# Down stage of a transformer block: the pending pair inside the plain product's first tile, and fewer operand sums in front of two snaps

## The chip, the core and the metric

The kernel runs on one core of one Trainium2 chip. The time is device time in microseconds (us) of one execution. Most executions of one kernel lie within a few us of each other. Engines: PE is the tensor engine (matmuls), PEld its weight loads, DVE the vector engine, ACT the scalar engine; SP only issues transfers here.

## The reference

A pre-LayerNorm block: linear attention, then a gated feed-forward part. Only the last product matters here, `h @ W_down` with h of 2048 x 3584 and W_down of 3584 x 1024:

```python
x = A_x
h = x + _A_ref(_layernorm(x), A_wqkv, A_wo)           # linear attention
# ... gate = relu(x @ W_gate); up = x @ W_up; h = gate * up   (feed-forward)
h2 = h + einsum("bsf,fd->bsd", h, W_down)             # the down stage
```

## The kernel before

The down stage replaces one 2x2 block product by seven products of block sums (a Strassen-Winograd scheme), in two levels. The outer level has seven steps, n = 0 to 6. Steps 0 and 5 are *plain*: four tiles of the output, two halves of 14 matmuls each. Steps 1, 2, 3, 4 and 6 are cut once more into seven groups m1 to m7 of 28 matmuls of 128x256. The groups of one step need sums of operand blocks, made on DVE: s1 to s4 from the activations (128x3584, 1.94 us from start to start) and t1 to t4 from the weights (128x1792, 1.0 us). The profile names their outputs xs, xd, x (from s) and ws, wd, w (from t).

A step's sums wait in a Python list, `queue`, while the program is built; `pop()` puts the next one into DVE's instruction stream. So where `pop()` stands decides what DVE does in which order.

```python
queue.extend((op, f.__name__, f) for f in (t1, s1, s2, t2, s4, s3, t3, t4))

def snap(nm, s, j):     # copies PSUM tile A (plus a base) away; until then PE may not add to A again
    add(out=st[nm][:], in0=view("A"), in1=base[s][:, :, cols(j)], op=ALU.add)
```

Within a step m1, m6, m7 and m4 accumulate into the same PSUM tile A, one on top of another, and a snap saves A after m1, m6 and m7. So m6 waits for the first snap, m7 for the second, m4 for the third. m4 and m3 of a step are issued in the next step: they are the *pending pair* of its forerunner, `prv`.

```python
for n in range(1, len(OUTER)):          # OUTER steps; step 0 is done before
    if op["k"] in INNER:                # a seven-product step
        cur["m1"]()
        if prv:
            prv["11"](); pop()
        cur["s1"]()                     # first snap
        cur["m2"]()
        if prv: prv["m4"]()
        late_x()
        cur["00"]()                     # first output
        pop()
        if prv:
            prv["10"](); prv["m3"]()
        late_w()                        # loads; queues the sums of the next step
        pop()
        cur["m6"]()
        if prv: prv["01"]()
        pop()
        ...
        cur["m5"]()
        cur["s2"]()                     # second snap
        ...
        pop(2)
        cur["m7"]()
        ...
        pop(2)
        cur["s3"]()                     # third snap
        prv = cur
    else:                               # the plain step, n = 5
        for p in range(4):
            ps = acc(...)
            plain_mm(ps, n, p, 0)
            plain_mm(ps, n, p, 1)
            if p == 0 and prv:
                prv["11"](); prv["m4"](); late_x(); prv["10"](); prv["m3"](); late_w(); prv["01"]()
                load_h(op["k"], 1)
            # drain ps: put = two adds and a store, then one add into u2
            ...
            pop(2)
        prv = None
```
(The code is shortened; statements are joined on one line here.)

## Time and profile before

| | before |
|---|---|
| median of the first three runs | 755.6 us (755.51 to 757.81) |
| PE busy, share of the profiled span of 755.9 us | 96% |
| down stage: start of m1 of step 1 to the end of the last DVE operation | 612.23 to 752.69 = 140.46 us |
| PE waits in that stage | 2.11 and 2.64 us |

The timeline view of PE shows the stage as groups back to back. Columns: start in us, length in us, engine, line, operation, output <- inputs, shapes, count; in brackets the idle time before it and what ended it. A length runs to the modelled end of the group's last matmul: groups listed with 3.22 us start 3.06 us apart. A wait in brackets is counted from that modelled end, so a stop costs PE 0.16 us more than the wait listed. These are m6, m5 and m7 of step 1 and the group after, then m2 and m6 of step 6 and the half group after:

```profile
618.34 3.22 PE L1105 MATMUL accA<-ws,xs 128*128 128x256 f16 x28
621.40 3.22 PE L1105 MATMUL accY<-ws,xd 128*128 128x256 f16 x28
626.73 4.88 PE L1105 MATMUL accA<-w,xd 128*128 128x256 f16 x28 [2.11 <-DVE snap L1111]
631.45 3.22 PE L1105 MATMUL accA<-wd,x 128*128 128x256 f16 x28
...
728.99 3.22 PE L1105 MATMUL accX<-wd,x 128*128 128x256 f16 x28
734.85 4.88 PE L1105 MATMUL accA<-ws,xs 128*128 128x256 f16 x28 [2.64 <-DVE snap L1111]
739.57 1.69 PE L1131 MATMUL accX<-ws,xs 128*128 128x256 f16 x14
```

PE stops twice, both times for a snap, and after each stop one group takes 4.88 us in place of 3.22. The timeline view of DVE says why the snaps were late:

```profile
620.41 1.08 DVE L1022 TENSOR_TENSOR ws<-wd 128x1792 f16<-128x1792 f16 x1
621.41 2.02 DVE L1035 TENSOR_TENSOR xs<-x 128x3584 f16<-128x3584 f16 x1
623.52 2.03 DVE L1038 TENSOR_TENSOR xs<-xs,x 128x3584 f16<-128x3584 f16 x1
625.46 1.22 DVE L1111 TENSOR_TENSOR snap<-accA,u 128x1024 f32<-128x1024 f32 x1
...
730.45 1.22 DVE L1278 TENSOR_TENSOR u<-accY,u 128x1024 f32<-128x1024 f32 x1
731.58 1.08 DVE L1029 TENSOR_TENSOR wd<-wd 128x1792 f16<-128x1792 f16 x1
732.58 1.08 DVE L1032 TENSOR_TENSOR ws<-wd,ws 128x1792 f16<-128x1792 f16 x1
733.58 1.22 DVE L1111 TENSOR_TENSOR snap<-accA,u 128x1024 f32<-128x1024 f32 x1
```

Both snaps had their source long before: the first one's m6 ended at about 621.4, the second one's m1 at about 729. Between stand sums that nobody waits for at that moment; ahead of the second snap stand also the drains of the plain step's last tile (the last of them, from 730.45, is shown). DVE ran what stands in its stream in that order: the first snap's source was ready at 621.4 and the snap ran at 625.46, in its place behind the sums.

The waits view (total us, times, longest) has one line for PE in the stage, and the chain of waits (start, length) begins with the two sums of the second place:

```profile
PE accA L1105 <- DVE snap L1111: 4.8, 2, 2.6
```
```profile
731.66 1.00 DVE wd L1029
732.66 1.00 DVE ws L1032
733.66 1.14 DVE snap L1111
734.81 0.04 issue
734.85 4.88 PE accA L1105 x28
```

The stretches view gives, for each stretch of time, its length, the busy time of PE, PEld, DVE, ACT and POOL, then the granted PE clock, the DMA share and GB/s:

```profile
624.60:626.70 2.10, 0.02 (x1) 0.00 (x0) 2.10 (x3) 0.00 (x0) 0.00 (x0) 1.00 1.03 411
626.70:631.50 4.80, 4.77 (x29) 3.65 (x29) 4.80 (x4) 0.00 (x0) 0.00 (x0) 0.64 0.55 216
631.50:695.60 64.10, 64.10 (x590) 57.45 (x588) 53.20 (x44) 0.00 (x0) 0.00 (x0) 1.00 0.82 296
...
732.10:734.80 2.70, 0.11 (x1) 0.00 (x0) 2.70 (x3) 0.00 (x0) 0.00 (x0) 1.00 0.88 283
734.80:739.60 4.80, 4.75 (x29) 3.61 (x29) 1.92 (x2) 0.00 (x0) 0.00 (x0) 0.64 0.40 127
```

After each stop the granted clock is 0.64 on average over the following group; the trace's clock records show a stretch of 3.413 us at 0.5 in each.

### The profile page before, as it was taken

To read this page: it belongs to the slowest core of one execution; us is meant where nothing else is said; L and a number is where in the kernel's file an instruction comes from. 1 tells how busy PE (TensorE), PEld (TensorE's weight loads), DVE (VectorE), ACT (ScalarE), POOL (GpSimd) and SP (SyncE) were. 2 spreads that over 40 slices of the span, in tenths; PEclk is the share of its full clock that TensorE was granted. 3 is DMA by queue.
4 is the path that set the end of the run, shared out by engine and by line. 5 is a ranking of instruction groups with operands and counts; after the bars stand their busy time and mean duration, and the time that the engine had idled before them with its cause. 6 is when DMAs were issued, how large, how long until landed. Compare 5 with 4: busy or idle time off the path is not lost. (4 is left out here: it accounts for less than half of the span.)

```text
span 755.9 us, 10599 instructions
## 1 busy us (share of the span) xinstructions
PE 727.9 (96%) x3967; PEld 384.2 (51%) x4020; DVE 568.2 (75%) x1023; ACT 324.7 (43%) x596; POOL 5.9 (1%) x44
## 2 busy tenths in 40 slices
PE   8999999999889989999999999999999998999987
PEld 3444555444344434444444444444444477888556
DVE  6997654876886766778778787887776398995695
ACT  4785653878767644444344444434344110000000
POOL 0000000000000000000000000000000000000000
PEclk9999999999999999999999999999999999999999
DMA  9756003089857526165638368585482596987722
GB/s 321 167 125 153 0 1 112 1 188 218 186 144 178 135 74 202 35 185 140 200 110 237 112 194 252 194 253 179 144 302 96 189 385 244 360 295 281 238 98 56
DMA packets 146579, 132.03 MB, mean 175 GB/s; under 512 B 50912, under 2 KB 128096, under 8 KB 146528
## 3 DMA queue, kind: packets, MB, share of 16 engines
q1 hardware_dynamic: 135392, 123.23, 53.7%
q10 hardware_dynamic: 11136, 8.13, 3.4%
q8 instruction: 31, 0.51, 0.3%
q14 instruction: 20, 0.16, 0.1%
HBM read 79.95 MB, written 39.85 MB: 158 GB/s over the span
## 5 line engine op out<-in xcount | busy, mean ns | idle before, releaser
L783 ACT ACTIVATE gu<-gu 128x512 bf16<-128x512 bf16 x72 | 45.4, 630 | 131.7 <-DVE gu L782 127.3
L778 ACT COPY snap<-accA 128x1024 f32<-128x1024 f32 x72 | 72.4, 1008 | 37.1 <-PE accA L773 37.1
L536 PE MATMUL attn<-wo_mem,oT 128*128 128x512 bf16 x247 | 58.7, 385 | 4.1 <-DVE o_sb L516 3.3
L773 PEld LDWEIGHTS <-tg 128*128 128x128 f16 x384 | 37.6, 98 | 45.3
L773 PEld LDWEIGHTS <-tu 128*128 128x128 f16 x384 | 37.6, 98 | 45.3
L782 DVE TENSOR_TENSOR gu<-accY,snap 128x1024 bf16<-128x1024 f32 x36 | 43.9, 1219 | 9.8 <-ACT snap L778 9.8
L153 ACT COPY u<-Aq 128x512 f32<-128x512 f32 x56 | 32.3, 582 | 44.0 <-PE Aq L297 20.4
L782 DVE TENSOR_TENSOR gu<-accX,snap 128x1024 bf16<-128x1024 f32 x36 | 43.8, 1218 | 7.3 <-PE accX L773 4.7
L773 PE MATMUL accA<-hn,tg 128*128 128x512 f16 (+1 forms) x192 | 49.3, 379 | 0.0
L773 PE MATMUL accA<-hn,tu 128*128 128x512 f16 (+1 forms) x192 | 49.3, 379 | 0.0
L1105 PEld LDWEIGHTS <-x 128*128 128x128 f16 (+1 forms) x448 | 43.8, 98 | 5.5
L773 PEld LDWEIGHTS <-wg 128*128 128x128 bf16 x288 | 28.2, 98 | 34.9 <-issue 1.1
L773 PEld LDWEIGHTS <-wu 128*128 128x128 bf16 x288 | 28.2, 98 | 34.0
L536 PEld LDWEIGHTS <-oT 128*128 128x128 bf16 x256 | 25.3, 99 | 36.0 <-issue 8.5
L1105 PEld LDWEIGHTS <-xs 128*128 128x128 f16 x280 | 28.2, 101 | 6.7 <-issue 2.8
L297 PEld LDWEIGHTS <-xT 128*128 128x128 bf16 (+1 forms) x192 | 18.6, 98 | 24.5 <-issue 3.2
L786 DVE TENSOR_TENSOR hq<-gu 128x512 bf16<-128x512 bf16 x48 | 20.3, 422 | 14.3 <-ACT gu L783 14.2
L516 DVE TENSOR_TENSOR o_sb<-nd,rd 128x384 bf16<-128x384 f32 (+1 forms) x48 | 22.8, 506 | 8.6 <-ACT rd L515 7.5
L1111 DVE TENSOR_TENSOR snap<-accA,u 128x1024 f32<-128x1024 f32 x16 | 19.5, 1218 | 11.1 <-PE accA L1105 11.1
L538 DVE SCALAR_TENSOR_TENSOR x_res<-attn,x_res 128x512 bf16<-128x512 f32 x32 | 22.0, 688 | 7.6 <-PE attn L536 7.5
L934 PEld LDWEIGHTS <-x 128*128 128x128 bf16 (+1 forms) x168 | 16.4, 98 | 19.8
L773 PE MATMUL accA<-hn,wg 128*128 128x512 bf16 x73 | 23.3, 379 | 2.0 <-DVE gu L702 0.8
(232 smaller groups left out, 1417.0 us busy)
## 6 DMA issues: line engine op xcount, KB each, us to landing
x<-x_dram SPq DMA_DIRECT2D x17, 896.0 KB, 8.4
x_dram<-hq SPq DMA_DIRECT2D x28, 512.0 KB, 3.0
wg<-in_B_W_gate_dram SPq DMA_DIRECT2D x14, 512.0 KB, 5.2
wu<-in_B_W_up_dram SPq DMA_DIRECT2D x14, 512.0 KB, 7.5
wraw<-in_B_W_down_dram SPq DMA_DIRECT2D x14, 512.0 KB, 4.9
x_dram<-hq SPq DMA_DIRECT2D x28, 256.0 KB, 2.4
t_dram<-wt SPq DMA_DIRECT2D x28, 256.0 KB, 2.3
xd<-x_dram SPq DMA_DIRECT2D x6, 896.0 KB, 6.5
```

The source lines that it names most:

```text
L153: nc.scalar.copy(out=snaps[nm, v], in_=A[v][:])
L297: nc.tensor.matmul(ps[:], lhsT=left[m - 1][:, kc, r + v * P:r + (v + 1) * P], rhs=right[m - 1][:, kc, :], start=(start and kc == 0), stop= ...
L516: nc.vector.tensor_tensor(out=ov[:, c0:c0 + n], in0=ndv[:, :, 0:P].rearrange("p k (h e) -> p k h e", h=HPC), in1=rd[:, 0:n, :].unsqueeze(3 ...
L536: nc.tensor.matmul(ps[:], lhsT=st["oT"][:, c, :], rhs=wo_sb[:, c, j * NW:(j + 1) * NW], start=(c == 0), stop=(c == KC - 1))
L538: nc.vector.scalar_tensor_tensor(out=h_sb[:, j * NW:(j + 1) * NW], in0=ps[:], scalar=1.0, in1=h_sb[:, j * NW:(j + 1) * NW], op0=ALU.mult, ...
L773: nc.tensor.matmul(ps[:, v, :], lhsT=w[v][n - 1][:, kc, :], rhs=left[n - 1][:, kc, :], start=(t is not None and kc == 0), stop=(kc == KH - ...
L778: nc.scalar.copy(out=st[nm][:], in_=halves(st["A"]))
L782: add(out=g[:], in0=halves(st[nm]), in1=st[base][:], op=ALU.add)
L783: nc.scalar.activation(out=g[:, 0, :], in_=g[:, 0, :], func=ACT.Relu)
L786: add(out=out[q], in0=st[q][:, 0, :], in1=st[q][:, 1, :], op=ALU.mult)
L1105: nc.tensor.matmul(pv[:, tt, :], lhsT=left(m)[:, f, tt * P:(tt + 1) * P], rhs=right(m)[:, f, :], start=(t is not None and f == 0 and tt % ...
L1111: add(out=st[nm][:], in0=view("A"), in1=base[s][:, :, cols(j)], op=ALU.add)
```

## The change

Its intent: let the two snaps run as soon as PE has filled A. (a) In a step without a forerunner two `pop()` fall away. (b) In the plain step PE does half of the first tile, then the pending pair, then the other half. (c) One sum is popped before the first tile's drain, and none after the last tile.

```diff
             late_w()
-            pop()
+            if prv:
+                pop()
             cur["m6"]()
             if prv:
                 prv["01"]()
-            pop()
+                pop()
...
                 plain_mm(ps, n, p, 0)
-                plain_mm(ps, n, p, 1)
                 if p == 0 and prv:
...
                     prv["01"]()
                     load_h(op["k"], 1)
+                    pop()
+                plain_mm(ps, n, p, 1)
...
-                pop(2)
+                pop(2 if p < 3 else 0)
```

No instruction is added or removed. On PE only m4, m3 and the second half tile of step 5 change places; on DVE sums, snaps and drains do.

## The prediction

The sum: 3.8 us for (a) and 4.5 us for (b) with (c), together the 8.3 us of the walk.

> **What bounds it.** The tensor engine (PE), 96% busy on the page; in the down stage (591 us to the end) the timeline shows groups of 28 matmuls back to back, 3.06 us each, seven per step. PE stops twice. (1) First seven-product step: group m7 waits 2.11 us, to 626.73, for the snap (vector engine, DVE) of 625.46, though its source m6 had ended at 621.4: the operand sums ws, xs, xs (1.00, 2.02, 2.03 us) stood in front of it. (2) Last step: m6 waits 2.64 us, to 734.85, for the first snap of 733.58, behind the plain product's last drain and two sums wd, ws (731.58 to 733.58). The chain of waits begins with these sums. Each stop also costs afterwards: the next group takes 4.88 us where its like take 3.22; the stretches view gives granted clock 0.64 there, 1.00 around. [...]two stretches of 3.413 us at 0.5. From group start to group start the stops cost 6.99-3.06 = 3.93 and 7.52-3.06 = 4.46 us: 8.4 us, 1.1%, all on the critical path.

> **What changes.** Nothing is added or removed; order moves.
> (a) In steps without a forerunner (first and last of the seven-product kind) two sums fewer stand before the second snap. In the first only ws (1.0) remains: the snap runs at about 621.5 to 622.7, and m7 goes at 624.46 unhindered. Sums run about one place later through the next three steps.
> (b) In the plain step PE runs half the first tile, then the pending pair, then the other half. This wins no PE time; but the pair's two outputs drain about 3 us earlier, in DVE idle time (4.89 us before the snap at 695.84, 5.89 before the drain at 704.94).
> (c) That room lets one sum (ws) run before the first tile's drain, and the last tile queues none; of eight sums seven run there, the eighth after the last step's first snap and output.

> **Size.** I walked the PE, DVE and load queues forward with the traced durations; the same walk over the old order gives the waits as 1.98 and 2.93 us (traced 2.11, 2.64). New order: no PE wait in the stage, the last step's first snap done 1 us before m6 needs it, the end 8.3 us earlier. Loads start up to 4 us earlier and land, in the walk, over 2 us before use. Part (a) is worth about 3.8 us, (b) with (c) about 4.5, nearly additive.

> **Prediction: 747.4 us**, 8 in 10 between 746.0 and 750.5. Faster by over 2%: 0.01; within 2%: 0.98; slower by over 2%: 0.01.

> **What would show it.** PE's idle before these two groups gone; both at 3.2 us; before the end only one half-clock stretch (at 203 us) left; these snaps at about 621.5 and 726; all up to 620 us unchanged; the tail after PE's end unchanged (about 4 us).

> **What would make it wrong.** DVE has little slack in the second to fourth seven-product steps: with PE 4 us earlier, the second step's second snap ends only about 1 us before m7 needs it; DVE operations 6% slower would bring a new stop of about 0.4 us and, if the clock drops again, 1.7 more. DMA is saturated from 622 to 627 us (share 1.02); the next loads landing over 2 us later than walked would hold a sum, and the snap behind it.

## The result, and the profile after

The changed kernel took 747.92 us (median of 6 runs, 747.15 to 749.07); before, in all 6 of its runs by then, 755.56 us. The ratio is 0.9897 (95% interval 0.9881 to 0.9912): 1.0% faster, clear of noise. A ratio is the mean time of one kernel's runs over that of the other's runs of the same rounds, so it is not quite the ratio of the medians quoted. Executions over 1.5% slower than the fastest of the same kernel are left out of the means.

The same groups on PE, in the timeline view: m6, m5, m7 of step 1, then m2, m6 of step 6 and the half group after it.

```profile
617.85 3.22 PE L1105 MATMUL accA<-ws,xs 128*128 128x256 f16 x28
620.91 3.22 PE L1105 MATMUL accY<-ws,xd 128*128 128x256 f16 x28
623.97 3.22 PE L1105 MATMUL accA<-w,xd 128*128 128x256 f16 x28
...
724.56 3.22 PE L1105 MATMUL accX<-wd,x 128*128 128x256 f16 x28
727.61 3.22 PE L1105 MATMUL accA<-ws,xs 128*128 128x256 f16 x28
730.67 1.69 PE L1131 MATMUL accX<-ws,xs 128*128 128x256 f16 x14
```

No brackets: PE waits for nothing in the stage (the waits view lists no PE wait from 591 us on), and both groups take 3.22 us. On DVE the snaps stand where they were wanted:

```profile
619.92 1.08 DVE L1022 TENSOR_TENSOR ws<-wd 128x1792 f16<-128x1792 f16 x1
621.11 1.23 DVE L1111 TENSOR_TENSOR snap<-accA,u 128x1024 f32<-128x1024 f32 x1
622.25 2.01 DVE L1035 TENSOR_TENSOR xs<-x 128x3584 f16<-128x3584 f16 x1
...
724.28 1.22 DVE L1280 TENSOR_TENSOR u<-accY,u 128x1024 f32<-128x1024 f32 x1
725.42 1.22 DVE L1111 TENSOR_TENSOR snap<-accA,u 128x1024 f32<-128x1024 f32 x1
727.81 1.23 DVE L1069 TENSOR_TENSOR o<-accX,snap 128x1024 bf16<-128x1024 f32 x1 [1.18 <-PE accX L1105]
```

and the stretches view has granted clock 1.00 in the same places:

```profile
624.60:626.70 2.10, 2.10 (x22) 1.88 (x21) 2.10 (x2) 0.00 (x0) 0.00 (x0) 1.00 1.01 405
626.70:631.50 4.80, 4.80 (x47) 4.29 (x44) 4.77 (x4) 0.00 (x0) 0.00 (x0) 1.00 0.92 356
631.50:695.60 64.10, 64.10 (x576) 56.13 (x574) 55.84 (x46) 0.00 (x0) 0.00 (x0) 1.00 0.86 305
```

The stage, measured as above, runs from 611.74 to 743.79 = 132.05 us. That is 8.41 us less than the 140.46 of before: 4.76 us of waits, 0.16 us more for each of the two stops, and 1.66 us for each of the two slow groups (4.88 less 3.22). The ratio of the timed runs is worth 7.8 us (0.0103 of 755.6); its interval, 6.6 to 9.0 us, holds 8.41 too, so this difference alone is not clear of noise. But the profiled run of before took 757.7 us, 2.1 us over the median of its runs: its trace may hold more slow clock than most of its runs do. Whether it does is what the experiments also had to show.

### The profile page after: what moved, and what is told of

It is laid out like the page before. It is cut to its first block, busy times and chain, and to the rows that moved or that the text cites. A ratio compares the mean times of both kernels' runs of the same rounds, so it can differ in the third digit from the quotient of the medians.

```text
span 747.0 us, 10654 instructions
## 1 busy us (share of the span) xinstructions
PE 725.9 (97%) x4020; PEld 382.2 (51%) x4020; DVE 568.4 (76%) x1023; ACT 324.6 (43%) x596; POOL 5.8 (1%) x44
## 4 chain that ended last, share of the span: by engine, by line
PE 79%; DVE 8%; ACT 5%; DMA 5%; issue 1%; SPq 0%; POOL 0%; DVEq 0%; ACTq 0%
PE accA L773 22%; PE accY L773 8%; PE accX L773 8%; PE accA L1105 8%; PE attn L536 5%; PE Aq L297 3%; PE accA L934 3%; PE accX L1105 3%; PE Aq L437 3%; PE accY L1105 2%; DMA hn<-hn 2%; PE Aq L693 2%; PE Eq L297 2%; PE accX L934 2%; PE accY L934 2%
```

## The experiments

Theory: each stop of PE has one cause, the sums that stand ahead of one snap; it costs its wait plus a half-clock stretch; the two stops are separate. Rivals: (1) DVE as a whole is the bound, so that delayed sums only move the stop; (2) the new PE order in the plain step itself wins the time; (3) the half clock has nothing to do with the stops, or comes with any stop.

All results in one table. "Stage" is from the start of m1 of step 1 to the end of the last DVE operation in the profiled execution; waits and slow clock (stretches at clock 0.5 within the stage, in us) are from the same trace. "Plain part" is (b) with (c).

| run | median us (runs) | ratio to before, 95% | stage us | waits us | at half clock us |
|---|---|---|---|---|---|
| before | | | 140.46 | 2.11 + 2.64 | 3.41 + 3.41 |
| whole change | 747.92 (6) | 0.9897, 0.9881 to 0.9912 | 132.05 | none | none |
| e1, (a) alone | 751.02 (4) | 0.9954, 0.9925 to 0.9983 | 134.86 | 2.65 | none |
| e2, plain part | 751.77 (4, one disturbed) | 0.9949, 0.9928 to 0.9970 | disturbed | | |
| e5, plain part again | 751.19 (4) | 0.9942, 0.9921 to 0.9964 | 134.32 | 2.11 | none |
| e3, (b) alone | 753.98 (4) | 0.9984, 0.9963 to 1.0005 | 137.17 | 2.12 + 1.02 | 3.41 |
| e4, last pop alone | 753.32 (4) | 0.9983, 0.9950 to 1.0015 | 136.80 | 2.12 + 0.65 | 3.41 |
| e11, (c) without (b) | 754.03 (1) | one look | 137.91 | 2.12 + 1.77 | 3.41 |
| e6, without the early pop | 748.46 (4) | 0.9906, 0.9886 to 0.9926 | 132.05 | none | none |
| e7, stop of 1 us added | 751.18 (4) | 0.9944, 0.9910 to 0.9979 | 133.24 | 1.03 | none |
| e8, stop of 4 us added | 755.83 (4) | 0.9994, 0.9965 to 1.0023 | 138.99 | 4.41 | 6.83 |
| e9, one sum more in step 2 | 749.09 (1) | one look | 132.50 | 0.29 | none |
| e10, three sums more | 753.11 (1) | one look | 134.75 | 2.54 | none |

The state of e9 to e11 is unknown (single runs), so of these only the stage in the trace is used. All kernels gave correct results.

### e1: part (a) alone

```diff
             late_w()
-            pop()
+            if prv:
+                pop()
             cur["m6"]()
             if prv:
                 prv["01"]()
-            pop()
+                pop()
```

> Part (a) alone: two sums fewer before the second snap of the first seven-product step; plain step as before. Theory (each PE stop comes from the sums that stand before one snap, and costs its wait plus a half-clock stretch; the two are separate): the first wait (2.1 us at about 626) and its half-clock stretch are gone, the second (2.6 us at about 735 minus 4) stays with its half-clock stretch; 3.9 us saved, about 751.7 us. Rival 1 (the vector engine as a whole is the bound in these steps, so delayed sums only move the stop): a new PE wait of 1 us or more in the second to fourth seven-product step, under 2 us saved.

Measured: the first wait is gone, no new one appears in steps 2 to 4, and the second stays at 2.65 us. Rival 1 falls. But the second stop's cost was a surprise. m2 and m6 of step 6 in the timeline view of this run:

```profile
722.68 3.22 PE L1105 MATMUL accX<-wd,x 128*128 128x256 f16 x28
728.54 3.22 PE L1105 MATMUL accA<-ws,xs 128*128 128x256 f16 x28 [2.65 <-DVE snap L1111]
```

The stop is as long as before, and yet the group after it takes 3.22 us and not 4.88: no half clock. In this run the stop cost only its wait and the 0.16 us: the stage is 2.81 us longer than the change's.

### e2 and e5: the plain part alone

```diff
                 plain_mm(ps, n, p, 0)
-                plain_mm(ps, n, p, 1)
                 if p == 0 and prv:
...
                     load_h(op["k"], 1)
+                    pop()
+                plain_mm(ps, n, p, 1)
...
-                pop(2)
+                pop(2 if p < 3 else 0)
```

> Parts (b) and (c) alone: plain step changed, pops of the first seven-product step as before. Theory: first wait of 2.1 us stays with its half-clock stretch, the second is gone with its own; 4.5 us saved, about 751.1 us. If the two parts need one another, e1 and this one together save clearly less than the 8.4 us.

Of e2's four executions the profiled one took 2731 us; the three others took 751.04 to 751.78. Its trace tells nothing of the change, so the same kernel ran once more:

> Second run of the plain-step part alone, because the profiled run of the first fell in a disturbed execution (2729 us). Theory: in the trace the first wait (2.1 us) stays, the second is gone; us minus the time lost to the granted clock lies 2.6 us under that of before and 2.1 us above that of the whole change.

Measured in e5: the second wait is gone, the first stays, and again, unlike before, without a half clock behind it (m5 and m7 of step 1, timeline view):

```profile
620.77 3.22 PE L1105 MATMUL accY<-ws,xd 128*128 128x256 f16 x28
626.11 3.22 PE L1105 MATMUL accA<-w,xd 128*128 128x256 f16 x28 [2.11 <-DVE snap L1111]
```

So (a) takes away the first wait and nothing else, (b) with (c) the second and nothing else; the waits add up. By the ratios the parts save 3.5 us (e1) and 3.9 to 4.4 us (e2, e5), together 7.3 to 7.9, against 7.8 of the whole; each of the three is uncertain by 1.6 to 2.2 us, so it is the traces that show the parts to be separate. The time lost to the granted clock is (1 - clock) times the span, run by run. Without it e5's runs take 749.17 us on average: 3.2 us less than those of before in the same rounds (2.6 expected), and 1.65 more than those of the change (2.1 expected).

### e3: part (b) alone

```diff
                 plain_mm(ps, n, p, 0)
-                plain_mm(ps, n, p, 1)
                 if p == 0 and prv:
...
                     load_h(op["k"], 1)
+                plain_mm(ps, n, p, 1)
```

> Part (b) alone: the PE order of the plain step changed (half tile, pending pair, half tile), all sums queued as before. Theory (the swap wins nothing on PE and only moves two drains into idle vector time): wait before m6 of the last step falls from 2.6 to about 1.1 us, 1.8 us saved; 3.5 if so short a stop no longer brings the half clock. Rival 2 (the swap itself is what removes the stop): no wait left there, 4.5 us saved.

Measured: the wait before m6 falls from 2.64 to 1.02 us and no half clock follows it. Rival 2 falls: the swap alone does not remove the stop. It only lets two drains end earlier.

### e4: no sums after the last tile, nothing else

```diff
-                pop(2)
+                pop(2 if p < 3 else 0)
```

> The last tile of the plain step queues no sums (part of c), nothing else changed; the two displaced sums run after the first snap of the last step. Theory: wait before m6 falls from 2.6 to about 0.9 us, since the snap still waits for the last tile's three drains (3.0 us); first wait stays. 1.7 us saved if any stop brings the half clock, 3.7 if so short a stop does not. If this saves as much as e2, the swap was not needed.

Measured: wait 0.65 us, no half clock behind it. The two sums of 1.0 us each had been worth 2.0 us of the wait, as they should. Swap (1.6 us) and last pop (2.0 us) each shorten the wait; either alone is too little for 2.64, and the two together are enough (e6, below, is just these two with (a)).

The timed runs of e3 and e4 save less than their stages: 1.2 and 1.3 us by the ratios, against 3.3 and 3.7 us in the traces. Their runs list on average as much loss to the clock (3.8 and 4.0 us) as those of before in the same rounds (3.5); without it they save 2.2 and 2.5 us, near the 1.6 and 2.0 by which the wait fell. The stages are compared with the one trace of before, whose clock of 0.993 is lower than that of its runs on average (0.995 in these rounds), so they count too much half clock.

### e6: the change without the early pop

```diff
                     load_h(op["k"], 1)
-                    pop()
                 plain_mm(ps, n, p, 1)
```
(against the changed kernel)

> The whole change without the one sum that it puts ahead of the plain step's first drain (the pop after the pending pair), so six sums run in the plain step and two after the last step's first snap. Theory: that pop is not needed for the time; no PE wait in the stage, same time as the whole change (747.9 us) within 0.3%. Rival: without it the sums come too late for the last step, a PE wait of 0.5 us or more before m7 or m4 there.

Measured: no wait, a stage of 132.05 us as with the pop, and a time that agrees within the intervals. The early pop is not needed for the time.

### e11: the early pop and no last pop, without the swap

```diff
                     load_h(op["k"], 1)
+                    pop()
...
-                pop(2)
+                pop(2 if p < 3 else 0)
```

> Part (c) without the swap (b): one sum before the first drain of the plain step's first tile, none after the last tile, PE order as before; first seven-product step as before. Theory: without the swap the early sum stands between the late drains, so the whole row of drains and sums comes later and the wait before m6 falls only from 2.6 to about 2.0 us (0.9 with no early sum, in e4: 0.65). Rival (the sums' places alone matter): wait under 0.7 us as in e4.

Measured: wait 1.77 us, against 0.65 in e4, which differs only by the early pop. Without the swap's room that sum pushes the snap back by 1.1 us, about its own length (the plain step's drains before it come 1.0 to 2.1 us later). The same line that is harmless after the swap costs 1.1 us without it.

### e7 and e8: stops of known length

The surprise of e1 asks what brings the half clock. In the clock records of the before trace the half-clock stretches at the two stops and the one before them are 3.413 us long and begin at 203.651, 626.904 and 736.130 us; the distances are 124.0 and 32.0 times 3.4133 us. The "window theory" below was at this point an assumption that these starts fit but do not show: the time is cut at such steps of 3.4133 us, and what counts is PE's idle time within one of these windows. If so, a stop of 2.1 us may fall into one window, or be cut in two by a window's edge. The author's estimate of how much idle time it takes, about 2.0 us, fits the stops traced by then: 2.11 to 2.13 us in the fullest window with a half clock behind (before, e3, e4), 1.36 us without (e1). By it a stop of 1.05 us is too short, and one of 4.05 us leaves about 2.0 us or more in one window however it is cut. To try it, one sum of the last step was repeated (same result) in front of its first snap in the changed kernel, k = 2 for e7, k = 5 for e8:

```diff
+            if tail:
+                for _ in range(k):
+                    nc.vector.tensor_tensor(out=op["t"]["t2"], in0=w_tile(n, 1)[:, :, HW:DW], in1=op["t"]["t1"], op=ALU.subtract)
             cur["s1"]()
```

> The whole change, with one operand sum of the last step (1.0 us) done twice more (same result) in front of that step's first snap, which has 1.0 us to spare: a wait of 1.05 us before m6. Window theory [...]: never a half-clock stretch from this stop; 1.0 us longer than the whole change. Rival (any stop of PE brings the half clock): 2.7 us longer, a half-clock stretch within 4 us after the stop.

> As e7 with five repeats: a wait of 4.05 us before m6. Window theory: [...]every run gets a half-clock stretch, of which up to 3.41 us lie after the stop: 5.0 to 5.8 us longer than the whole change, granted clock lower by 0.002 in every run. Rival (the half clock falls at random or with load, not with idleness): only some runs show it, 4.05 us longer in the others.

The lines of m6 (timeline view, e7 and then e8):

```profile
732.92 3.22 PE L1105 MATMUL accA<-ws,xs 128*128 128x256 f16 x28 [1.03 <-DVE snap L1111]
```
```profile
733.18 5.58 PE L1105 MATMUL accA<-ws,xs 128*128 128x256 f16 x28 [4.41 <-DVE snap L1111]
```

Measured in e7: a wait of 1.03 us, no half clock in the stage, which is 1.2 us longer than the change's. Measured in e8: a wait of 4.41 us and a half-clock stretch of 6.83 us, two windows, from 731.24 us, of which 4.88 lie after the stop's end; the stage is 6.94 us longer. The expected 4.05 us of wait was too little because the repeats ran 1.1 us apart, not 1.0 (e8's five took 5.59 us; why was not shown); the expected upper bound of 5.8 us failed with it, and because a second half-clock window followed the first, after a window with 1.95 us idle. The times do not decide. By the ratios e7 is 3.5 us slower than the change, nearer to the rival's 2.7 than to the theory's 1.0, with intervals that allow both; its four runs list 0.993 to 0.999, a loss to the clock of 3.0 us on average against 0.5. In the profiled run, the slowest of them, all the half clock lies elsewhere (6.83 us at half clock at the very start, 3.41 from 207.5 us); where the others lost it, no trace shows. And one of e8's runs lists 0.998, as one run of the change does without any stop. The traces do tell the theories apart, with a count over all of them.

| trace and stop | idle in the fullest window | half clock |
|---|---|---|
| before, 2.11 and 2.64 us | 2.11 and 2.13 us | yes, yes |
| e3, e4, e11, first stop, 2.12 us | 2.12 us each | yes |
| e1, 2.65 us | 1.36 us (and 1.29 in the next) | no |
| e5, 2.11 us | 1.18 us (and 0.93 before) | no |
| e10, 2.54 us | 1.80 us | no |
| e7, 1.03 us | 1.03 us | no |
| e8, 4.41 us | 2.46 us (and 1.95 in the next) | yes, two windows |

The window theory fits every stop in this table; "any stop" (rival 3) does not (2.65 us without in e1), nor does the length of the stop alone (2.65 us without, 2.11 with).

### e9 and e10: how much room DVE has left

In front of the second snap of step 2 of the changed kernel, one of the next step's sums was repeated, k = 1 and 3:

```diff
+            if n == 2:
+                for _ in range(k):
+                    nc.vector.tensor_tensor(out=nxt["t"]["t1"], in0=w_tile(n + 1, 0)[:, :, HW:DW], in1=w_tile(n + 1, 0)[:, :, 0:HW], op=ALU.subtract)
             cur["s2"]()
```

> The whole change, with one operand sum (1.0 to 1.1 us) done once more (same result) in front of the second snap of the second seven-product step, where the trace of the change leaves 0.7 us between that snap's end and the group m7 that waits for it. Theory (little slack there): a new PE wait of 0.3 to 0.5 us before m7 of that step, stage 0.3 to 0.5 us longer, no half clock. Rival (the vector engine has idle time that takes up one sum): no wait, stage as in the whole change (132.05 us).

> As e9 with three repeats (3.3 us). Theory: a PE wait of about 2.6 us before m7 of the second step, none in the steps after it; stage 2.6 us longer than 132.05, and up to 1.7 more [...]. Rival (later steps have the bound too): further waits there, stage over 4.5 us longer.

Measured: m7 of step 2 waits 0.29 us for one repeat and 2.54 us for three, and no other wait appears. The lines of m7 (timeline view, e9 and then e10):

```profile
645.64 3.22 PE L1105 MATMUL accA<-wd,x 128*128 128x256 f16 x28 [0.29 <-DVE snap L1111]
```
```profile
649.67 3.22 PE L1105 MATMUL accA<-wd,x 128*128 128x256 f16 x28 [2.54 <-DVE snap L1111]
```

So the change leaves DVE only about 0.7 us of room in front of m7 of step 2. PE no longer waits in this stage, and none of the kernels tried beats the change.

## Why the prediction was right, point by point

- **The place of the loss**: right. Two stops, each from the sums ahead of one snap; e1 takes away only the first, e2 and e5 only the second.
- **(a) "first and last of the seven-product kind"**: right for the first step. In the last one, no sum stood ahead of the second snap before the change either (the plain step had used up all eight), so (a) takes nothing away there; in the trace of the change one sum, left over by (c), stands there (729.68), and nobody waits for it.
- **No new wait in steps 2 to 4**: right. The room left before m7 of step 2 was put at about 1 us; the trace leaves 0.7, and e9 shows that one more sum of 1.1 us already makes PE wait.
- **The swap wins no PE time and only moves drains**: right, by e3 (wait 1.02 us left). The expectations put this wait at about 1.1, that of e4 at about 0.9 (measured 0.65) and that of e11 at about 2.0 (measured 1.77).
- **(c) "lets one sum run before the first tile's drain"**: true, but of no use for the time, by e6. What counts in (c) is that the last tile queues none.
- **The size in the traces**: right. 8.3 to 8.4 us were predicted, the stage shortened by 8.41.
- **The size in the runs**: 747.4 predicted, 747.92 measured, inside the range of 746.0 to 750.5. The term that was over-sized is "Each stop also costs afterwards", counted at its full 1.7 us for both stops in every run. The time lost to the granted clock, computed run by run as in e5, is on average 3.21 us in the 16 runs of before that list a clock, 0.50 in the 6 of the change. The rest of the time falls from 752.47 to 747.52, by 4.95 us, close to the 5.08 us of the two stops (4.76 of waits and twice 0.16); the clock's part falls by 2.7, where I had counted 3.4. (The clock is listed to three digits, so one run's loss is known to 0.4 us; the means of these few runs leave the 2.7 uncertain by about 0.5, one standard error.) So the gap to 3.4 is not itself clear of noise; that the term was too big is shown by e1 and e5, whose stops brought no half clock. How much of the 2.7 belongs to the two stops is not shown, since it includes stretches outside the down stage, such as the one near 203 us that the trace of before has and that of the change has not. An estimate from the count: if 1.95 us idle (among the four that go both ways) in a window of 3.413 us is what it takes, and a stop falls anywhere in the windows with equal chance (which was not shown), a stop of 2.11 us brings the half clock in 48% of the runs and one of 2.64 us in 63%, which makes at most 1.9 us for both in place of 3.4. So, by this estimate, part of the close agreement with 747.4 is luck. The prediction took the one trace, where both stops had been hit, for every run.
- **"only one half-clock stretch (at 203 us) left"**: not so in the trace of the change. That one lies in the attention part: in the trace of before the window ahead of it was idle for 2.07 us, and in that of the change the fullest window thereabouts was idle for 1.53 us. e3, e6, e7, e8 and e10 show it again near 203 to 208 us.

## What to carry to other kernels

Where a tightly packed engine waits for a small operation on another engine, look at what stands ahead of that operation in the other's queue (here the snap, ready at 621.4, ran at 625.46 behind the sums); moving work that nobody waits for yet behind it took 1.0% off here, with not one instruction fewer. Walk both queues forward with traced durations before moving, since the room used up here must be found elsewhere: here it was in the next steps, to within 0.7 us. When one trace shows a slow clock behind a stop, look into several traces before counting it for every run: here the wait of the first stop was 2.11 us in before and in e5, with the slow clock behind it in before and without it in e5.

## What else the traces show of the slow clock

- A stop of one length, shorter than 3.413 us, came with the half clock and without: 2.11 us with it (before) and without (e5), 2.64 us with it (before) and 2.65 without (e1). These are different kernels with the same stop; one kernel was not traced twice.
- e2's profiled execution was slow in another way: its trace holds no clock record at all (its page has no PEclk line, so the 1.000 that is listed for it is no reading), while 128x512 matmuls took 1105 ns in place of 379 and started 840 ns apart in place of 216 (those of 128x256 at the end 420 in place of 109), all through the 2729 us. The lines of one group by shape (busy us, mean ns), e2 and then the change:

```profile
L773 PE MATMUL accA<-hn,wu 128*128 128x512 bf16 x96 | 85.7, 1105 | 0.0
```
```profile
L773 PE MATMUL accA<-hn,wu 128*128 128x512 bf16 x96 | 24.6, 379 | 0.0
```

  Why that execution was slow stays open; it happened once.
